# An MLP whose first group has three chunks in the program's order, four early pieces in a Fourier stage, and staged first transfers

## The chip, the cores and the metric

The kernel runs on one core of one Trainium2 chip. The metric is device time in microseconds (us) of one execution of the whole program. TensorE does the matmuls, VectorE and ScalarE the elementwise work (both can read PSUM), GpSimd (POOL) elementwise work in SBUF, and SyncE (SP) and ScalarE issue most DMA transfers. Each engine has one queue of instructions and works them off in order; engines wait for each other through semaphores.

## The reference

Three blocks are computed one after the other, for batch B = 4, S = 576 positions, 8 heads of 64, so a model width of 512. All inputs and the output are float32.

```python
# attention with a bias from relative positions
psi_rel = log1p(abs(pos[:, None] - pos[None, :]))
psi_i = log1p(maximum(pos[:, None], 1.0))
h = maximum((psi_rel / psi_i)[..., None] @ w1 + b1, 0.0)      # 32 hidden
scores = q @ k^T / 8 + (h @ w2).transpose(2, 0, 1)
x = softmax(scores) @ v                                        # [B, S, 512]
# Fourier mixing, normalisation, MLP
u = x + real(fft(fft(x, axis=1), axis=2))
mu = mean(u); var = mean((u - mu) ** 2)
un = (u - mu) / sqrt(var + 1e-06)
x = u + maximum(un @ w_ch1, 0.0) @ w_ch2                       # 512 -> 2048 -> 512
# gated block
h = maximum(x @ w_in, 0.0); a, v = halves of h
v_s = w_spatial @ normalised(v) + b_spatial
out = (a * v_s) @ w_out
```

## The kernel before, in words

One program does the three blocks in stages. Matmuls that need float32 accuracy are done on split operands: x = hi + lo in a fast 32-bit format, and hi*hi + hi*lo + lo*hi are accumulated, so that one product is three matmuls.

**Bias stage** (`bias_phase`, 0 to about 137 us). 48 blocks of three groups of four positions. For each group a 0/1 mask [128, 576] is made, on one of three ways (`ROUTE`): by TensorE and ScalarE from chunks of `c_xb` (X), by VectorE (D) or by POOL and VectorE (P) from `win` and `bn`. `make` makes a mask three blocks ahead, `collect` multiplies masks with `g` on TensorE, `evict` scales with `xt` and adds. `xscale` scales `xt` in place, 72 columns at every fourth block. The first transfers are issued at the top: `w`, a first `c_xb` chunk, `bn` and the two parts of `xt` on SP, `win` on ScalarE's queue. `win` is scaled by VectorE (L212) before the first D and P masks.

**Attention stage** (to about 433 us). At its end `first_folds` lets VectorE and ScalarE begin the folds for the Fourier stage: up to two steps for each round, up to step `F_MAX`. A batch has six steps, numbered on through the batches.

**Fourier stage** (`fft_phase`, about 422 to 518 us). For each batch b and parity e: `stage1` multiplies folded rows with cosine and sine tables (tile y, copied from PSUM by ScalarE, L826), `second` multiplies the copies (tile D, copied as d), `residual` transposes every second column of x on TensorE (tile xs, L843), and VectorE adds both into `ut` (L859, and `mirror`, L866). `step()` is called between these parts; it counts, takes one fold step, and, where `XPLAN` says so, one step of `extra`, the generator `early` of `tail`: preparing the first MLP weights and the mean of chunk 0. This stage and the one before stand under `manual_schedule`, which keeps the order of the program on each engine; elsewhere the scheduler of the language chooses an order.

**MLP stage** (`mlp_phase`, about 519 to 962 us). The 2304 positions are nine chunks of 256 (`MC`); the hidden width is 16 blocks (f) of 128. An item is one (f, chunk): 12 matmuls into `h` (L1227), `gh` = relu on ScalarE (L1231), `gl` = the rest on VectorE (L1232), and, two items later (`LAGF`), 12 matmuls into the chunk's `acc` (L1263). Chunks come in groups: (0, 1), then single ones, then (7, 8). A group's closing pieces multiply `acc` by the chunk's factor and add it to `ut` (L1273, L1274). `h` rotates over three PSUM tiles, and the statistics have a fourth tile, `st`.

A chunk must be normalised: `means` (three adds and a matmul with ones), `center`, `split` (uh, ul), `squares`, and `factor` (a matmul with ones, L1157, and the root). These are generators; an item takes some of their steps. In the first group the 32 weight tiles of 512 KB come in as well. `Weights.step` moves each weight in flight on by one: a transfer into one of three stage buffers, two steps later a ScalarE copy `wsq` (L958), then three VectorE integer passes (L962, L966, L969) that make a float32 from 64-bit input, then `wh` on ScalarE (L974) and `wl` on POOL (L975). Four weights (`N_EARLY` = 2 blocks) are made early. The stage buffers also hold a chunk's centred values `uc` while it is normalised.

**Gate stage** (to 1178 us). Its weights are prepared in the MLP's last group, through `later`.

Of the kernel before, what the change touches and what calls it, by code (L numbers as in the profile page):

```python
# [104 lines left out]
def bias_phase(tc, nc, io, vs, bias, biasl, early, es):  # L105
# [106 lines left out]
    nc.vector.tensor_scalar(out=win, in0=win, scalar1=w1p, scalar2=None, op0=ALU.mult)  # L212

# [456 lines left out]
F_MAX = 9  # L670
YB = 2
XPLAN = {10: 1, 14: 1, 30: 1, 31: 1, 32: 1}
# [125 lines left out]
def fft_phase(tc, nc, folds, tabs, ut, bank, extra, es):  # L798
# [35 lines left out]

    def residual(b, e, y):

        x = xs[b]
# [36 lines left out]
    def step():  # L874
# [3 lines left out]
        for _ in range(XPLAN.get(count, 0)):  # L878
            next(extra, None)
# [4 lines left out]
    for b in range(B):  # L884
        for e in range(2):
# [4 lines left out]
            for n, nm in enumerate(group):  # L890
# [3 lines left out]
                step()  # L894
                if n == 1:
# [91 lines left out]
LAGF = 2  # L987
MC = 256
# [97 lines left out]
class Norm:  # L1086
# [17 lines left out]
    def means(self, c, bank, stage, keep=None):  # L1104

        nc, u = self.nc, self.chunk(c)
        self.uc[c] = self.room(stage)
        s = self.uc[c][:, 0]
# [8 lines left out]
        if keep:  # L1117
            self.mean[c] = self.pool.tile([128, MC], F32, tag=keep, name="mu", bufs=1 + (keep == "rs"))
            nc.scalar.activation(out=self.mean[c], in_=m, func=AF.Copy)
            if keep == "rs":  # L1120
                self.scale[c] = self.mean[c]
        yield

    def center(self, c):

        uc, u = self.uc[c], self.chunk(c)
# [4 lines left out]
    def split(self, c, pool):  # L1131

        nc, uc = self.nc, self.uc[c]
        uh = pool.tile([128, 4, MC], F32R, tag="uh", name="uh", bufs=2)
        ul = pool.tile([128, 4, MC], F32R, tag="ul", name="ul", bufs=2)
# [17 lines left out]
    def factor(self, c, bank):  # L1153
# [4 lines left out]
        if c not in self.scale:  # L1158
            self.scale[c] = self.pool.tile([128, MC], F32, tag="rs", name="rs", bufs=2)
# [7 lines left out]
def mlp_phase(tc, nc, io, ut, norm, W, wts, later, es):  # L1167
# [11 lines left out]
    for _ in zip(norm.center(0), norm.split(0, lp)):  # L1179
        pass  # L1180

    for group in [(0, 1)] + [(c,) for c in range(2, NCH - 2)] + [(NCH - 2, NCH - 1)]:
        first, last = 0 in group, NCH - 1 in group
        pair = len(group) == 2
        c = group[-1] + 1

        def before():

            for x in group:
                if x != group[0]:  # L1190
                    yield from norm.means(x, bank, wts.stage)
                    yield from norm.center(x)
                    yield from norm.split(x, lp)
# [13 lines left out]
        if pair:  # L1207
            n = N_EARLY
            items = [(f, 0) for f in range(n)] + [(f, 1) for f in range(n)] + items[2 * n : -4]
            items += [(f, x) for x in range(2) for f in range(NF - 2, NF)]  # L1210
        acc = [ps_c.tile([128, len(group), MC], F32, tag=f"acc{d}", name="acc") for d in range(4)]
        gs = {}
        for i in range(len(items) + LAGF):
            if i < len(items):
# [7 lines left out]
                h = ps_h.tile([128, 512], F32, tag="h", name="h")  # L1222
                n = 0
                for k in range(4):
                    q = slice(128 * k, 128 * k + 128)
                    for st, mv in ((w1h, uh), (w1h, ul), (w1l, uh)):
                        nc.tensor.matmul(out=h[:, 0:MC], lhsT=st[:, q], rhs=mv[:, k], start=(n == 0), stop=(n == 11))  # L1227
# [3 lines left out]
                nc.scalar.activation(out=gh, in_=h[:, 0:MC], func=AF.Relu)  # L1231
                nc.vector.scalar_tensor_tensor(  # L1232
                    out=gl, in0=h[:, 0:MC], scalar=0.0, in1=gh.bitcast(F32), op0=ALU.max, op1=ALU.subtract
                )
# [450 lines left out]
```

## Time and profile before

| what | value |
|---|---|
| median of three runs | 1182.06 us (1177.35 to 1182.33) |
| the profiled execution's own time | 1180.53 us |
| its span, first to last instruction | 1178.6 us |
| TensorE matmuls busy | 1075.7 us, 91% of the span |
| VectorE busy | 716.2 us, 61% |
| ScalarE busy | 569.4 us, 48% |
| POOL busy | 379.0 us, 32% |
| mean granted TensorE clock | 0.974 |

The times of the trace are counted from the span's start. A busy share is that of the whole span and is made up of stages with different limits: the table by stretch below shows more. The granted clock is that which TensorE was allowed, as a share of 2.4 GHz; its other level is 1.2 GHz.

### The profile page before, as it was taken

Reading aid. Unit: us, or ns where it says so; the run is one execution under the profiler, and the core shown is the slowest. Engines: PE = TensorE matmul, PEld = TensorE weight load, DVE = VectorE, ACT = ScalarE, POOL = GpSimd, SP = SyncE. Lnnn points to the kernel's source line nnn. Section 1 sums busy time; section 2 is a strip of 40 time slices with the busy share of each in tenths; the row PEclk is TensorE's granted clock in tenths of the full one; section 3 lists DMA queues with packets and bytes.
Section 4 is the critical chain, followed back from the end, with each engine's and each line's share of the span. In section 5 each row is a group of like instructions: output and inputs, shape, how many; then the busy total and the mean of one; then the engine's idle time right before and its main releaser. Section 6 shows DMA issues by size and latency. Waiting matters only on the chain.

```text
span 1178.6 us, 25594 instructions
## 1 busy us (share of the span) xinstructions
PE 1075.7 (91%) x10519; PEld 989.0 (84%) x10519; DVE 716.2 (61%) x1887; ACT 569.4 (48%) x1056; POOL 379.0 (32%) x316
## 2 busy tenths in 40 slices
PE   4999898888988869989889999999999999999998
PEld 2778787777877757778779999999999999898997
DVE  4998877767877785579995242342567245443522
ACT  2888898798877623345542221221234224333332
POOL 2677687677777400014540000000014211101010
PEclk7999999989999969999999999999999999999999
DMA  6442088978998951015630000000214000101001
GB/s 153 162 131 96 12 168 180 165 166 171 184 169 159 201 168 37 1 37 171 187 108 1 1 1 1 1 1 1 73 37 147 11 1 1 37 1 45 1 36 45
DMA packets 142320, 96.34 MB, mean 82 GB/s; under 512 B 111416, under 2 KB 122812, under 8 KB 141948
## 3 DMA queue, kind: packets, MB, share of 16 engines
q1 hardware_dynamic: 139192, 85.85, 31.1%
q10 hardware_dynamic: 2724, 5.90, 1.7%
q0 software_dynamic: 288, 2.97, 0.7%
q8 instruction: 82, 1.34, 0.5%
q14 instruction: 34, 0.28, 0.1%
HBM read 58.42 MB, written 9.14 MB: 57 GB/s over the span
## 4 chain that ended last, share of the span: by engine, by line
PE 55%; DVE 18%; DMA 9%; ACT 5%; issue 5%; POOL 5%; SPq 1%; ACTq 0%; POOLq 0%; DVEq 0%
PE h L1227 14%; PE acc L1263 14%; PE psp L1398 5%; PE pu L1373 4%; PE po L1420 4%; DMA pt<-hl 3%; PE pv L1321 3%; PE sc L412 3%; POOL hl L464 2%; DMA raw<-in_k 2%; DVE wsq L966 2%; PE y L823 2%; DVE bt L308 2%; DMA win<-in_c_win 2%; DVE mask L232 2%
## 5 line engine op out<-in xcount | busy, mean ns | idle before, releaser
L975 POOL TENSOR_TENSOR wl<-wsq,wh 128x512 fp32r<-128x512 f32 x44 | 67.1, 1528 | 428.7 <-DVE w L1149 259.3
L1263 PE MATMUL acc<-gl,wh 128*128 128x256 f32 x576 | 162.8, 283 | 10.4 <-DVE gl L1232 10.0
L1263 PE MATMUL acc<-gh,wh 128*128 128x256 f32 x576 | 163.9, 286 | 2.7 <-ACT gh L1231 2.6
L1232 DVE SCALAR_TENSOR_TENSOR gl<-h,gh 128x256 fp32r<-128x256 f32 x144 | 60.2, 421 | 172.6 <-ACT gh L1231 172.5
L1227 PE MATMUL h<-uh,wh 128*128 128x256 f32 x576 | 162.9, 284 | 2.4 <-ACT uh L1137 2.4
L1227 PE MATMUL h<-uh,wl 128*128 128x256 f32 x576 | 162.9, 283 | 1.8 <-POOL wl L975 1.8
L1227 PE MATMUL h<-ul,wh 128*128 128x256 f32 x576 | 162.8, 283 | 0.6 <-DVE ul L1138 0.6
L1263 PE MATMUL acc<-gh,wl 128*128 128x256 f32 x576 | 161.8, 281 | 0.0
L1231 ACT ACTIVATE gh<-h 128x256 fp32r<-128x256 f32 x144 | 54.6, 380 | 213.9 <-PE h L1227 213.7
L518 PE MATMUL po<-vp,pt 128*128 128x65 f16 (+1 forms) x2240 | 95.6, 198 | 29.5 <-DMA pt<-hl 25.9
L1263 PEld LDWEIGHTS acc<-gl,wh 128*128 128x128 f32 x576 | 109.6, 190 | 13.3 <-DVE gl L1232 13.0
L464 POOL TENSOR_TENSOR hl<-P,hl 128x1024 f16<-128x1024 f32 x92 | 116.5, 1292 | 11.3 <-ACT hl L458 9.7
L518 PEld LDWEIGHTS <-pt 128*128 128x128 f16 (+1 forms) x2240 | 81.8, 103 | 44.3 <-DMA pt<-hl 31.4
L1227 PEld LDWEIGHTS h<-uh,wh 128*128 128x128 f32 x576 | 111.1, 193 | 3.4 <-ACT uh L1137 3.2
L1263 PEld LDWEIGHTS acc<-gh,wh 128*128 128x128 f32 x576 | 109.5, 191 | 4.7 <-ACT gh L1231 4.3
L1227 PEld LDWEIGHTS h<-uh,wl 128*128 128x128 f32 x576 | 110.7, 192 | 2.2 <-POOL wl L975 2.2
L1227 PEld LDWEIGHTS h<-ul,wh 128*128 128x128 f32 x576 | 110.7, 192 | 0.9 <-DVE ul L1138 0.8
L1263 PEld LDWEIGHTS acc<-gh,wl 128*128 128x128 f32 x576 | 109.6, 190 | 0.1
L447 ACT ACTIVATE P<-s,mm 128x576 f32<-128x576 f32 x144 | 103.3, 765 | 7.1 <-DVE mm L440 6.6
L425 DVE CUSTOM_DVE_ANT_0 s<-sc,lowb 128x576 f32<-128x576 f32 x80 | 60.6, 757 | 30.7 <-PE sc L412 26.6
L264 PE MATMUL bps<-g,mask 128*128 128x64 f16 x1152 | 61.6, 195 | 17.7 <-DVE mask L319 11.7
L247 ACT ACTIVATE mask<-pre 128x576 f16<-128x576 f32 x96 | 60.9, 651 | 31.2 <-PE pre L244 29.8
(247 smaller groups left out, 2778.8 us busy)
## 6 DMA issues: line engine op xcount, KB each, us to landing
w<-in_w_ch SPq DMA_DIRECT2D x32, 512.0 KB, 3.5
vld<-in_v ACTq DMA_DIRECT2D x16, 320.0 KB, 3.0
raw<-in_v SPq DMA_DIRECT2D x16, 320.0 KB, 3.4
raw<-in_q SPq DMA_DIRECT2D x16, 288.0 KB, 3.7
raw<-in_k SPq DMA_DIRECT2D x16, 288.0 KB, 6.0
w<-in_w_in SPq DMA_DIRECT2D x8, 512.0 KB, 3.5
out<-o SPq DMA_DIRECT2D x16, 256.0 KB, 2.0
xd<-x SPq DMA_DIRECT2D x15, 256.0 KB, 7.5
```

Of the source, the lines that this page charges most:

```text
L247: nc.scalar.activation(out=m.rearrange("p (x e) -> p x e", x=2), in_=p[:, :, 0:288], func=AF.Sigmoid, scale=1e30)
L264: nc.tensor.matmul(out=full(ps, it // 2)[:, it % 2, :, gi], lhsT=ms[gi][:, 128 * it : 128 * it + 128], rhs=g[:, k], start=(k == 0), stop=( ...
L425: nc.vector.tensor_tensor_reduce(out=s.rearrange("p (x e) -> p x e", x=2), in0=sc[:, :, 0:288], in1=bv.rearrange("p (x e) -> p x e", x=2), ...
L447: nc.scalar.activation(out=P[:, x], in_=s, func=AF.Exp, bias=mm[:, 1, x : x + 1], scale=1.0)
L464: nc.gpsimd.tensor_tensor(out=hl[:, :, o : o + c], in0=P[:, :, j : j + c], in1=hl[:, :, j : j + c], op=ALU.subtract)
L518: nc.tensor.matmul(out=po[c, t % 4, 0:w], lhsT=pt[:, x, c], rhs=vp[:, j, hh, f : f + w], start=(i == 0), stop=(i == len(seq) - 1),)
L975: nc.gpsimd.tensor_tensor(out=lo, in0=w[4], in1=hi.bitcast(F32), op=ALU.subtract)
L1227: nc.tensor.matmul(out=h[:, 0:MC], lhsT=st[:, q], rhs=mv[:, k], start=(n == 0), stop=(n == 11))
L1231: nc.scalar.activation(out=gh, in_=h[:, 0:MC], func=AF.Relu)
L1232: nc.vector.scalar_tensor_tensor(out=gl, in0=h[:, 0:MC], scalar=0.0, in1=gh.bitcast(F32), op0=ALU.max, op1=ALU.subtract)
L1263: nc.tensor.matmul(out=acc[d][:, x], lhsT=st[:, q], rhs=mv, start=(i == LAGF and n == 0), stop=(i == len(items) + LAGF - 1 and n == 2),)
L1398: nc.tensor.matmul(out=p[:, 0:CH], lhsT=st, rhs=mv, start=(n == 0), stop=(n == len(seq) - 1))
```

## The change

1. **First transfers.** At the top only the first 72 columns of `xt` are requested. The other 504 columns and the second `c_xb` chunk are issued further down, after the scaling of `win`: a memset of xt's last column, which stands behind that scaling on VectorE, makes the transfer wait.
2. **Fourier stage.** `F_MAX` is 5 instead of 9. `extra` is taken one step at every count from 8 on (`X_FIRST`), and `early` first makes the four weights and then the means of the first three chunks, each kept in its own tile. From the fourth (b, e) on, `gather` copies the columns that `residual` will transpose into contiguous room, on ScalarE.
3. **MLP.** The first group has three chunks (`TOGETHER`) and stands under `manual_schedule`. Norm steps are taken eight at an item for the first six items; a weight is started at item 0, then at two of three items up to 15, then at each. `h` has two PSUM tiles of two halves: blocks 0 and 1 of three in the one, block 2 and the statistics in the other. `acc` is two tiles for each chunk, over six tags in turn. The closing pieces go by chunk.

```diff
-    for k in (slice(0, 72), slice(72, S)):
-        nc.sync.dma_start(out=xt[:, :, k], in_=io["c_x"][:, :, k])
-    fill(1)
+    nc.sync.dma_start(out=xt[:, :, 0:72], in_=io["c_x"][:, :, 0:72])
...
     nc.vector.tensor_scalar(out=win, in0=win, scalar1=w1p, scalar2=None, op0=ALU.mult)
+
+    nc.vector.memset(xt[:, :, S - 1], 0.0)
+    nc.sync.dma_start(out=xt[:, :, 72:S], in_=io["c_x"][:, :, 72:S])
+    fill(1)
...
-F_MAX = 9
+F_MAX = 5
-XPLAN = {10: 1, 14: 1, 30: 1, 31: 1, 32: 1}
+X_FIRST = 8
...
+    room = xs[0].rearrange("p t f -> p (t f)")
+    parts = {}
+
+    def gather(b, e):
+
+        n = 2 * b + e
+        if 3 <= n < 2 * B:
+            o = 1280 * (n % 2)
+            t = parts[n] = room[:, o : o + 1280].rearrange("p (t s c) -> p t s c", t=5, s=2)
+            for s in range(2):
+                col = 257 + e if s else e
+                nc.scalar.activation(out=t[:, :, s], in_=xs[b][:, :, col : col + 255 : 2], func=AF.Copy)
...
-                nc.tensor.transpose(t[:, s, 128 * n : 128 * n + r], x[0:r, k, c], ident[0:r, 0:r])
+                i = x[0:r, k, c] if near is None else near[0:r, k, s]
+                nc.tensor.transpose(t[:, s, 128 * n : 128 * n + r], i, ident[0:r, 0:r])
...
-        for _ in range(XPLAN.get(count, 0)):
+        if count >= X_FIRST:
             next(extra, None)
...
                 step()
+                if n == 0:
+                    gather(b + e, 1 - e)
...
+TOGETHER = 3
...
-    def center(self, c):
+    def center(self, c, stage=None):
+        if c not in self.uc:
+            self.uc[c] = self.room(stage)
...
-    ps_h = es.enter_context(pool(tc, name="ps_h", bufs=3, space=PSUM))
+    ps_h = es.enter_context(pool(tc, name="ps_h", bufs=1, space=PSUM))
     ps_c = es.enter_context(pool(tc, name="ps_c", bufs=1, space=PSUM))
-    ps_l = es.enter_context(pool(tc, name="ps_l", bufs=1, space=PSUM))
+    halves = [ps_h.tile([128, 2, MC], F32, name=f"h{x}") for x in range(2)]
+    hs = [halves[0][:, 0], halves[0][:, 1], halves[1][:, 0]]
     def bank():
-        return ps_l.tile([128, 512], F32, tag="st", name="st")
+        return halves[1][:, 1]
...
-    for group in [(0, 1)] + [(c,) for c in range(2, NCH - 2)] + [(NCH - 2, NCH - 1)]:
+    for group in [tuple(range(TOGETHER))] + [(c,) for c in range(TOGETHER, NCH - 2)] + [(NCH - 2, NCH - 1)]:
+        es1 = ExitStack()
+        if 0 in group:
+            es1.enter_context(tc.manual_schedule())
...
-        acc = [ps_c.tile([128, len(group), MC], F32, tag=f"acc{d}", name="acc") for d in range(4)]
+        acc = {}
+        for x in range(several):
+            for z in range(2):
+                acc[x, z] = ps_c.tile([128, 2, MC], F32, tag=f"acc{turn % (2 * TOGETHER)}", name="acc")
+                turn += 1
...
-                h = ps_h.tile([128, 512], F32, tag="h", name="h")
+                h = hs[i % 3]
...
-                busy = pair and not (group[1] in norm.scale and group[1] not in norm.uc)
-                for _ in range(4 if busy else 1):
+                busy = several > 1 and not (group[-1] in norm.scale and group[-1] not in norm.uc)
+                for _ in range(8 if busy and i < 2 * several else 4 if busy else 1):
                     next(todo, None)
                 if first:
-                    wts.step(not busy or i < 2)
-                    while not busy and wts.busy() and (min(f + WLEAD, NF - 1), x) not in W:
-                        wts.step()
+                    wts.step(i == 0 or i > 2 and (i % 3 != 2 or i > 15))
...
     def early():
-        for _ in range(2):
-            wts.step()
-            yield
-        yield from norm.means(0, bank[0], wts.stage, "mu")
-        while len(W) + wts.wants() < 2 * N_EARLY:
+        while len(W) < 2 * N_EARLY:
             wts.step(len(W) + len(wts.flight) < 2 * N_EARLY)
             yield
+        for c in range(TOGETHER):
+            yield from norm.means(c, bank[0], wts.stage, f"mu{c}")
```

## Rows read from the trace of the kernel before

**Rows 1.** Busy time by stretch: PE, PEld, DVE, ACT, POOL, clock, DMA share, GB/s
```profile
24.50:31.10 6.60, 6.58 (x84) 5.08 (x84) 4.91 (x12) 2.92 (x5) 1.23 (x1) 0.52 0.04 14
440.40:492.00 51.60, 51.30 (x275) 40.53 (x276) 32.13 (x55) 16.95 (x34) 2.59 (x2) 0.97 0.07 21
519.00:636.40 117.40, 101.64 (x778) 96.35 (x779) 101.74 (x172) 53.98 (x112) 43.76 (x28) 0.97 0.38 117
636.40:865.40 229.00, 229.00 (x1943) 228.45 (x1942) 87.58 (x231) 47.44 (x128) 0.00 (x0) 1.00 0.03 10
865.40:962.00 96.60, 94.31 (x779) 93.44 (x778) 48.42 (x96) 36.69 (x82) 29.28 (x27) 0.98 0.20 60
...
519.00:540.00 21.00, 17.69 (x122) 16.51 (x123) 19.48 (x45) 12.47 (x29) 4.11 (x3) 0.92 0.26 76
```

**Rows 2.** Chain that ended last, first 40 us: start, length, what
```profile
1.69 18.37 DMA win<-in_c_win
...
20.08 0.83 DVE win L212
...
24.52 0.39 PE bps L264 x4
...
36.07 0.69 DVE xt L217
```

**Rows 3.** DMA view of the first 40 us: rate in 40 slices
```profile
GB/s 0 17 141 268 340 208 229 235 222 229 215 167 204 177 205 173 190 191 266 261 113 105 108 97 90 39 5 0 16 0 0 0 0 46 282 8 16 88 290 390
```

**Rows 4.** Timeline 428 to 441, VectorE, ScalarE, TensorE: start, length, what, idle before
```profile
428.45 1.48 DVE L746 TENSOR_TENSOR lowb<-lowb 128x1280 f32<-128x1280 f32 x1
429.96 0.82 DVE L753 TENSOR_TENSOR raw<-lowb 128x635 f32<-128x635 f32 x1
...
432.69 0.35 DVE L533 TENSOR_SCALAR ri<-po,vs 128x4 f32<-128x4 f32 x2
...
430.90 0.74 ACT L755 ACTIVATE fhi<-raw 128x640 fp32r<-128x640 f32 x1 [4.31 <-DVE raw L754]
...
440.36 0.85 PE L823 MATMUL y<-tt,fhi 128*128 128x290 f32 x2 [4.28 <-ACT y L826]
```

**Rows 5.** Timeline of the Fourier stage, VectorE and TensorE
```profile
456.76 0.76 DVE L859 TENSOR_TENSOR lowa<-xs,d 128x578 f32<-128x578 f32 x1 [3.70 <-ACT d L857]
...
470.49 0.76 DVE L859 TENSOR_TENSOR lowa<-xs,d 128x578 f32<-128x578 f32 x1
...
491.87 1.40 PE L843 MATMUL xs<-ident,lowb 128*128 128x128 f32 x6 [0.16 <-DVE lowa L859]
```

**Rows 6.** Timeline of TensorE: transposes of strided and of contiguous columns
```profile
457.76 1.34 PE L843 MATMUL xs<-ident,raw 128*128 128x128 f32 x6
...
403.14 0.74 PE L487 MATMUL turn<-ident,P 128*128 128x128 f32 x5
```

**Rows 7.** Groups by line, 519 to 636.4 us: busy, mean ns, idle before
```profile
L969 DVE SCALAR_TENSOR_TENSOR wsq<-w,wsq 128x512 int32<-128x512 int32 x28 | 38.4, 1370 | 0.5
L966 DVE SCALAR_TENSOR_TENSOR wsq<-w,wsq 128x512 int32<-128x512 int32 x28 | 20.3, 725 | 0.6
L962 DVE TENSOR_SCALAR wsq<-wsq 128x512 int32<-128x512 int32 x28 | 13.2, 472 | 1.0 <-ACT wsq L958 0.9
...
L975 POOL TENSOR_TENSOR wl<-wsq,wh 128x512 fp32r<-128x512 f32 x28 | 43.8, 1563 | 59.9 <-ACT wh L974 59.9
...
L974 ACT ACTIVATE wh<-wsq 128x512 fp32r<-128x512 f32 x28 | 17.7, 634 | 36.1 <-DVE wsq L969 36.0
```

**Rows 8.** Timeline of one item in a single-chunk group
```profile
700.97 0.28 PE L1227 MATMUL h<-uh,wl 128*128 128x256 f32 x1
...
701.70 0.42 DVE L1232 SCALAR_TENSOR_TENSOR gl<-h,gh 128x256 fp32r<-128x256 f32 x1 [2.29 <-ACT gh L1231]
```

**Rows 9.** Timeline: a matmul of statistics, and four norm pieces in a row
```profile
524.67 0.59 PE L1157 MATMUL st<-w,ones 128*128 128x256 f32 x2
...
693.89 1.40 DVE L1128 TENSOR_TENSOR w<-lowa,st 128x256 f32<-128x256 f32 x4
```

More of the change, by code (lines that the diff above doesn't have):

```diff
@@ L1106, in means @@
         nc, u = self.nc, self.chunk(c)
-        self.uc[c] = self.room(stage)
-        s = self.uc[c][:, 0]
+        t = self.room(stage)
+        s = t[:, 0]
+        if not keep:
+            self.uc[c] = t
         nc.vector.tensor_tensor(out=s, in0=u[:, 0], in1=u[:, 1], op=ALU.add)
@@ L1170, in mlp_phase @@
     gp = es.enter_context(pool(tc, name="mg", bufs=LAGF + 1))
-    ps_h = es.enter_context(pool(tc, name="ps_h", bufs=3, space=PSUM))
+    ps_h = es.enter_context(pool(tc, name="ps_h", bufs=1, space=PSUM))
     ps_c = es.enter_context(pool(tc, name="ps_c", bufs=1, space=PSUM))
-    ps_l = es.enter_context(pool(tc, name="ps_l", bufs=1, space=PSUM))
+    halves = [ps_h.tile([128, 2, MC], F32, name=f"h{x}") for x in range(2)]
+    hs = [halves[0][:, 0], halves[0][:, 1], halves[1][:, 0]]
     def bank():
-        return ps_l.tile([128, 512], F32, tag="st", name="st")
+        return halves[1][:, 1]
     NCH = B * S // MC
-    for _ in zip(norm.center(0), norm.split(0, lp)):
+    for _ in zip(norm.center(0, wts.stage), norm.split(0, lp)):
         pass
-    for group in [(0, 1)] + [(c,) for c in range(2, NCH - 2)] + [(NCH - 2, NCH - 1)]:
+    turn = 0
+    for group in [tuple(range(TOGETHER))] + [(c,) for c in range(TOGETHER, NCH - 2)] + [(NCH - 2, NCH - 1)]:
+        es1 = ExitStack()
+        if 0 in group:
+            es1.enter_context(tc.manual_schedule())
         first, last = 0 in group, NCH - 1 in group
-        pair = len(group) == 2
+        several = len(group)
         c = group[-1] + 1
         def before():
[L1189 to L1193, printed above, removed]
+            for x, y in zip(group, group[1:] + (None,)):
+                if y is not None:
+                    if y not in norm.mean:
+                        yield from norm.means(y, bank, wts.stage)
+                    yield from norm.center(y, wts.stage)
+                    yield from norm.split(y, lp)
                 yield from norm.squares(x)
@@ L1206, in mlp_phase @@
         items = [(f, x) for f in range(NF) for x in range(len(group))]
[L1207 removed]
+        if several > 1:
             n = N_EARLY
[L1209 to L1211 removed]
+            items = [(f, x) for x in range(several) for f in range(n)] + items[several * n : -2 * several]
+            items += [(f, x) for x in range(several) for f in range(NF - 2, NF)]
+        acc = {}
[3 more added lines that the diff above has]
+                turn += 1
         gs = {}
@@ L1226, in mlp_phase @@
                     for st, mv in ((w1h, uh), (w1h, ul), (w1l, uh)):
-                        nc.tensor.matmul(out=h[:, 0:MC], lhsT=st[:, q], rhs=mv[:, k], start=(n == 0), stop=(n == 11))
+                        nc.tensor.matmul(out=h, lhsT=st[:, q], rhs=mv[:, k], start=(n == 0), stop=(n == 11))
                         n += 1
@@ L1263, in mlp_phase @@
                         nc.tensor.matmul(
-                            out=acc[d][:, x], lhsT=st[:, q], rhs=mv,
-                            start=(i == LAGF and n == 0), stop=(i == len(items) + LAGF - 1 and n == 2),
+                            out=acc[x, d // 2][:, d % 2], lhsT=st[:, q], rhs=mv,
+                            start=(e == 0 and d % 2 == 0 and n == 0), stop=(e == NF - 1 and d % 2 == 1 and n == 2),
                         )
@@ L1268, in mlp_phase @@
                     later(e)
-        for d in range(4):
-            for x, cc in enumerate(group):
-                p = acc[d][:, x]
+        es1.close()
+        for x, cc in enumerate(group):
+            for d in range(4):
+                p = acc[x, d // 2][:, d % 2]
                 o = ut[:, d, MC * cc : MC * cc + MC]
```

21 lines of the change are left out of this document (10 added, 11 removed).

## The prediction

> **What bounds the kernel now.** I read the page first: TensorE is busy 91% of the span, so a gain has to come from stretches where it waits or runs at the lower clock. The table of busy time by stretch gives these [rows 1]. From 636.4 to 865.4 us TensorE never waits: 80 items (one hidden block of one chunk, 24 matmuls) in 229.0 us, 2.862 us an item, 1.43 us for its h half and 1.43 for its acc half. From 519.0 to 636.4 it does 32 items, which at that pace are 91.6 us, in 117.4, and VectorE is busy 101.7 of these: 25.8 us lost. The last pair, 865.4 to 962.0, loses 5. From 440.4 to 492.0 it is busy 51.3 of 51.6 us. Ahead of the MLP the chain of waits shows two more places: TensorE's first real work starts at 24.52 us, behind a transfer of win that takes 18.37 us [rows 2]; and at 440.36 us it has waited 4.28 us for ScalarE's copy of y [rows 4]. The change reaches all three.
>
> **Staged first transfers.** win shares the DMA engines with the rest of xt (1260 KB) and the second chunk of c_xb. After the change those wait for a VectorE memset that stands behind the scaling of win. What is left ahead of it (w, wx, bn, win, the first c_xb chunk, 72 columns of xt) is by their shapes about 1690 KB; adding up the DMA rate us by us, that much had moved by 9.3 us [rows 3]. So win lands near 9.8 and its scaling runs near 10.4, behind that of bn, instead of 20.08: 9.7 us. All that follows (POOL's z, the compare, TensorE's start 4.44 us after the scaling) moves with it. TensorE's pause then is 2 us instead of 11.6, and the stretch 24.5 to 31.1, where the granted clock was 0.52 (mostly its lower level of 1.2 GHz), should run higher; there VectorE's 4.9 busy us of 6.6 become the bound [rows 1]: 1.7 us more. Against it: the rest of xt now starts near 12 us, with two c_xb chunks behind it; 2412 KB at the 220 KB per us of these rows are 11 us, so it lands by 23. Block 4's scaling of xt asks for it: at 36.07 before, 11.5 us after TensorE's start [rows 2], so at 14.8 + 11.5 - 1.7 = 24.6. That is little cover, with v's loads beside it; I charge 0.6. Sum 9.7 + 1.7 - 0.6: **-11** (bounds -4, if VectorE stands 7 us waiting for xt, and -12).
>
> **Fourier stage.** F_MAX 5 takes four of batch 1's fold steps out of the attention tail: two sums of 1.48 us and two pieces of 2.73 (429.96 to 432.69), 8.4 us of VectorE [rows 4]. ScalarE waits 4.31 us for one of them, and the copies of y, for which TensorE waits, stand behind it in its queue. So TensorE should be 8.5 us earlier in batch 0. But the steps are not gone: they move behind, and the four early weights, of which two were prepared in gaps before this stage, now have their turn at counts 8 to 15, in batch 1. There VectorE has no room: from the output add at 456.76 to that at 470.49 it never waits for long, and the next transposes start right after such an add (at 491.87 even 0.16 us late) [rows 5]. Before the second add stand three weights now, each three integer passes of 0.47, 0.73 and 0.69 to 1.37 us [rows 7], with POOL's subtraction beside them 2.4 on average: 7.2 us. So of 8.5 about 1 is left at 471, and, with the means' adds (nine of 0.35 us) in the queue, nothing at 492. The last 27 us hold no folds, so there TensorE's own work counts: gather makes the transposed columns contiguous. Six strided transposes take 1.34 us, a pitch of 0.21; five of contiguous columns in the attention stage 0.74, a pitch of 0.117 [rows 6]: 0.57 us for a call of residual, five such calls that show after 492: 2.9. One more mean matmul costs 0.59 [rows 9]. The ten ScalarE gathers lie beside waits of ScalarE; uncovered they would cost 7. Sum **-2.5** (bounds -9, if weights and folds fit; +4, if neither the tail's gain nor the gathers show).
>
> **MLP, first group.** Three chunks make 48 items, 137.4 us, for the same 28 weights. VectorE's work: 28 weights of 2.45 (their three rows with the overlap of neighbours) are 69, 48 gl of 0.37 18, normalising chunks 1 to 3 some 51 pieces of 0.35, 18: 105 us, so VectorE is no longer the bound over the group. What is lost lies in the order.
>
> *Items 0 to 5.* In the program's order the factor matmul (st) stands in TensorE's queue between h and acc, and waits for that chunk's squares; eight norm steps follow each item. Count from the end of the first h, with VectorE pieces at 0.35 us [rows 9] and gh, gl ending 0.87 us after h [rows 8]. The first st waits for gh, then gl, 4 centers, 4 subtractions, gl, 3 adds (0.45 + 13 x 0.35): ready at 5.0 us, TensorE, with one h done, at 2.35: 2.7 lost. It ends at 5.6. The second waits for 18 more pieces (6.3) and ScalarE's root with handovers (2.3, an estimate): ready 14.2; TensorE, after the read of st, h, acc and h, at 10.4: 3.8. The third, from 14.8, for 10 pieces and one weight (3.5 + 1.7): ready 20.0, TensorE, after acc and h, 17.7: 2.3. With three st of 0.6 and 1.4 us for shared banks (below) 12 us are lost, where before the first 21 us held 122 matmuls, some 14 us of work [rows 1].
>
> *Weights at a fixed pace.* Up to f = 7 the step that ends a weight comes in the item just before its first use: ScalarE's wh (0.63) after gh, then POOL's wl (1.56) [rows 7] end 2.3 to 2.7 us after h, while the next h wants wl at 1.43 + 0.24 = 1.67: about 0.9 us, five times: 4.5. From item 16 one weight an item keeps VectorE at 2.45 + 0.37 = 2.82 of 2.862 us: 1.5 us for jitter.
>
> Its first h runs at the lower clock, as before (0.92 granted over the first 21 us, 1.7 us lost). So the group takes 137.4 + 1.7 + 12 + 4.5 + 1.5 = 157.1 us. The same three chunks took 117.4 + 45.8 = 163.2: -6.1.
>
> *h in shared banks.* h had three tiles; now blocks 0 and 1 of three lie in one tile and block 2 in another with the statistics. If accesses of two engines to one bank must take turns, every third h waits until gl of the one before has been read: 0.87 us after its end, with an acc half of 1.43 between: 0.56 us of room [rows 8]. Where VectorE is free it costs nothing; a group's start has no acc between, and there it costs up to 1.2 us. I take 1 us for the first group's end and 3 for the five later groups (none if tracked by bytes). MLP -6.1 + 4: **-2** (bounds -20, with the second case and no such waits, and +16, with the first).
>
> The Trainium skill, "PSUM — Partial Sum Buffer", section "PSUM bank collisions raise a hardware error", says that two engines must not be in one bank and quadrant at once, even at different columns, so such accesses have to be ordered by bank. No row of before shows h and gl in one bank; by that rule the waits are there, and without it the sum would be some 5 us lower.
>
> **Sum.** The profiled execution took 1180.53 us: 1180.5 - 11 - 2.5 - 2 = 1165. Its time is 1.5 us under the median of the three runs, so I say **1166**.
>
> **Rivals.**
> 1. *VectorE is late where banks are shared (not faster).* For: between 519 and 636 VectorE was 87% busy, and three pieces of a weight (2.5 us) can stand ahead of a gl. From the point where gl ends over 1.43 us after its h, every third h waits. Price: 1 us at each of 7 such items from 16 to 36 and 5 in the last group, 12; the first group's 24 closing pieces (8.3 us) ahead of the next gl, 5; four later starts of 1.2, 5; less the 4 charged: +18, 1184. Against: gl comes before the weight's pieces in each item, and the later groups are free to be ordered around it.
> 2. *TensorE isn't held at the start (faster still).* If adds and squares run ahead further than one piece per 0.35 us lets me count, the first six items lose 4 instead of 12, and wl is in time: -13, 1153. For: the pair lost only 7 there. Against: one queue, one order.
> 3. *xt comes too late (the staging doesn't do what it says).* The loads of v, 320 KB each, and the second and third c_xb chunk share the engines with it; if it lands at 30 us, 6 to 7 us of the 11 are gone: 1173. Against: the rate above.
>
> **Chances.** Forecast (1157 to 1177) 0.52; first rival (1176 to 1195) 0.16, second 0.20, third 0.12. Under 0.5%, some 6 us, a measurement here can't tell from no change. Faster by more than that (under 1176): 0.50 + 0.20 + 0.08 = 0.78; within it (to 1188): 0.02 + 0.09 + 0.04 = 0.15; slower 0.07, all from the first rival. The range leaves out about a tenth on either side: 1147, inside the second rival's case, to 1181, inside the first's.
>
> **What would show it.** Right: scaling of win near 10.4 and the first compare-fed matmuls near 15; xt's second scaling without a long wait; the copy of y no longer 4 us late; the output add of batch 1 behind three weights' passes; st in TensorE's queue with waits of 2 to 4 us, three times; the first acc of the fourth chunk some 156 to 160 us after the first h. Wrong: VectorE waiting for xt over 3 us in block 4; h waiting for gl in the single-chunk groups (229.0 us for five chunks becoming over 46.5 a chunk); or first items without waits for st.

## The result and the profile after

The changed kernel takes 1192.9 us (median of four runs, 1191.1 to 1194.7) where the kernel before, beside it, takes 1182.2: a ratio of 1.0096, 95% interval 1.0068 to 1.0125. It is slower by about 1%; 1166 was forecast. The profiled execution took 1191.71 us with a span of 1189.9.

The program has four seams that are easily found in any trace: TensorE's first mask product, its first product with the single column p1 (the Fourier stage begins), the first h of the MLP, and the first pv of the gate stage. The stretches between them, read from the timelines (from the first mask product to p1 the executions profiled here differ by up to 9 us, 397.7 to 406.7, where the code is the same, so that the stages are compared and not the ends):

| us | before | forecast | after |
|---|---|---|---|
| to the first mask product | 24.5 | 14.8 | 18.2 |
| from it to p1 | 398.0 | 397 | 397.7 |
| p1 to first h | 96.4 | 93.9 | 101.0 |
| first h to pv (MLP) | 442.1 | 440 | 456.1 |
| pv to the end | 217.6 | 217.6 | 217.0 |

The start's gain is smaller than forecast, the Fourier stage's is a loss, and 14 us are lost in the MLP. Rows of after, first by stretch (columns as in [rows 1]):

```profile
18.20:24.80 6.60, 6.60 (x98) 5.20 (x98) 5.41 (x14) 3.04 (x6) 1.69 (x2) 0.68 0.84 330
448.80:516.89 68.09, 55.05 (x288) 40.52 (x286) 38.00 (x63) 25.95 (x50) 6.47 (x4) 0.90 0.06 16
516.89:551.40 34.51, 24.02 (x128) 22.23 (x129) 20.53 (x54) 13.88 (x36) 1.28 (x1) 0.75 0.11 31
551.40:599.00 47.60, 43.32 (x361) 41.61 (x359) 28.49 (x48) 16.76 (x35) 11.78 (x9) 1.00 0.37 112
599.00:653.00 54.00, 48.91 (x410) 47.62 (x410) 51.45 (x69) 26.69 (x51) 30.11 (x17) 1.00 0.49 147
686.10:871.60 185.50, 184.79 (x1553) 184.08 (x1552) 69.00 (x180) 38.62 (x103) 0.00 (x0) 1.00 0.04 12
871.60:972.95 101.35, 94.49 (x777) 93.12 (x775) 50.23 (x100) 36.37 (x82) 26.90 (x27) 0.98 0.19 57
```

The first row answers to 24.50:31.10 before: granted clock 0.68 instead of 0.52. The second is the Fourier stage from D of (1, 0) (the product D of batch 1, parity 0) to the first h: TensorE idle for 13 of 68 us. The same stretch of before, with 1.7 us idle:

```profile
464.22:518.95 54.73, 53.05 (x284) 40.75 (x282) 31.38 (x51) 18.68 (x38) 2.99 (x2) 1.00 0.06 20
```

The third is the first six items of the MLP: 34.5 us, clock 0.75. In the fifth VectorE is busy 51.45 of 54 us, with 17 weights and 17 gl: 3.03 us for a weight and a gl. The last pair, 96.6 before [rows 1], takes 101.4.

**Start.** VectorE's timeline of after, and the DMA view of 7 to 13 us (the line DMA is the busy share of the 16 engines in tenths, in 40 slices):

```profile
13.76 0.82 DVE L210 TENSOR_SCALAR win<-win,w 128x1148 f32<-128x1148 f32 x1 [3.40 <-DMA win<-in_c_win]
...
28.89 0.77 DVE L219 TENSOR_SCALAR xt<-xt,gs 128x360 f32<-128x360 f32 x1
```
```profile
DMA  3303212403223312223213221332212321022100
...
DMA packets 254, 0.52 MB, mean 87 GB/s; under 512 B 149, under 2 KB 149, under 8 KB 254
...
q10 hardware_dynamic: 108, 0.48, 20.9%
```

The scaling of win comes at 13.76 instead of 20.08 [rows 2], not at 10.4. The second scaling of xt waits for nothing. From 7 to 13 us, just before win is there, it is nearly alone (q10: 0.48 of 0.52 MB) and moves at only 80 KB per us (87 with the rest), with 20.9% of 16 engines' time: as much as 3.3 engines.

**Fourier stage.** Timelines of after, three engines:

```profile
455.02 0.43 DVE L981 TENSOR_SCALAR wsq<-wsq 128x512 int32<-128x512 int32 x1
455.48 0.69 DVE L985 SCALAR_TENSOR_TENSOR wsq<-w,wsq 128x512 int32<-128x512 int32 x1
456.21 0.69 DVE L988 SCALAR_TENSOR_TENSOR wsq<-w,wsq 128x512 int32<-128x512 int32 x1
...
459.22 1.27 DVE L760 TENSOR_TENSOR fhi<-lowb,fhi 64x128 fp32r<-64x128 f32 x1
...
462.30 0.75 DVE L876 TENSOR_TENSOR lowa<-xs,d 128x578 f32<-128x578 f32 x1
```
```profile
463.09 0.64 ACT L879 ACTIVATE d<-D 1x580 f32<-1x580 f32 x1 [2.69 <-DVE lowa L876]
463.64 0.61 ACT L993 ACTIVATE wh<-wsq 128x512 fp32r<-128x512 f32 x1
464.16 1.46 ACT L849 ACTIVATE raw<-lowb 128x640 f32<-128x640 f32 x2
```
```profile
464.98 1.80 PE L860 MATMUL xs<-ident,raw 128*128 128x128 f32 x6 [9.24 <-ACT raw L849]
```

To here the transition had worked: D of (1, 0) began at 448.80 instead of 464.22, 6.6 us of it by the earlier start and 8.8 in this stage (32.9 us from p1 instead of 41.7). Then TensorE waits 9.24 us for a gather, which stands in ScalarE's queue behind the second copy of d, which waits for VectorE's output add, which stands behind the passes of three weights (one of them is shown) and two folds. Two smaller waits follow: 1.81 us at 476.62, for VectorE's adds, before the matmul of a mean, and 1.99 before the first h (1.38 before). D of (1, 0) to the first h takes 68.1 us, before 54.7 (518.95 - 464.22).

**MLP.** Waits of TensorE, 517 to 686 us and then 686.1 to 973:

```profile
PE h L1179 <- DVE w L1171: 8.8, 3, 3.1
PE h L1261 <- POOL wl L994: 4.7, 5, 1.3
PE h L1261 <- DVE gl L1266: 4.4, 6, 0.9
PE h L1261 <- ACT uh L1159: 2.0, 1, 2.0
...
PE h L1261 <- DVE gl L1266: 6.7, 3, 3.9
PE h L1179 <- DVE w L1183: 0.8, 1, 0.8
```

Each line gives the total, the number of waits and the longest. L1179 is the matmul of statistics in its shared tile: three waits of 2.6 to 3.1 us. After the first group, only h waiting for gl counts.

### The profile page after: what moved, and what is told of

It reads as the page before. It is cut to its first block, busy times and chain, and to the rows that moved or that the text cites. A ratio compares the mean times of both kernels' runs of the same rounds, so it can differ in the third digit from the quotient of the medians.

```text
span 1189.9 us, 25620 instructions
## 1 busy us (share of the span) xinstructions
PE 1079.8 (91%) x10519; PEld 990.1 (83%) x10519; DVE 718.4 (60%) x1888; ACT 576.6 (48%) x1068; POOL 379.0 (32%) x316
## 4 chain that ended last, share of the span: by engine, by line
PE 47%; DVE 12%; issue 3%; ACT 3%; POOL 1%; DMA 1%; DVEq 0%; ACTq 0%; POOLq 0%; SPq 0%
PE h L1261 14%; PE acc L1296 12%; PE psp L1432 5%; PE pu L1407 4%; PE po L1454 4%; PE pv L1355 3%; PE y L825 3%; DVE wsq L985 2%; DVE wsq L988 2%; PE D L872 2%; DVE wsq L981 1%; PE xs L860 1%; DVE gl L1266 1%; POOL wl L994 1%; DMA w<-in_w_in 1%
## 5 line engine op out<-in xcount | busy, mean ns | idle before, releaser
L1261 PE MATMUL h<-uh,wh 128*128 128x256 f32 x576 | 166.2, 289 | 15.0 <-DVE gl L1266 11.1
```

The source lines that it names most:

```text
L1261: nc.tensor.matmul(out=h, lhsT=st[:, q], rhs=mv[:, k], start=(n == 0), stop=(n == 11))
```

## The experiments

Ratios are to the kernel before, beside it on the same chip. Where a kernel has one profiled run, its stages are compared.

**1. The staged transfers alone.** The kernel before with the first two parts of the diff above (`xt` in two transfers, the second behind the memset).

> The kernel before with the staged first transfers alone. Theory A (what the profile of after shows at the start is a lasting gain, and everything else lost it): TensorE's first mask product starts at about 18.2 us instead of 24.5, each later stage is 6 to 7 us earlier, the end too: 1175 to 1176 us. Rival B (the rest of xt, landing later, or the lower clock takes some of it back by the end of the stage): under 3 us of gain, 1179 or more. The forecast's step said 11 us: 1171.

Measured: 1176.7 us, ratio 0.9925 (0.9897 to 0.9953); first mask product at 18.38, p1 to first h 97.4, MLP 443.5. The gain lasts: theory A. Its 9 us (0.0075 of 1182) have an interval of 5.6 to 12, so the trace's 6.1 are the better number.

**2. No gathers.**

```diff
-        if 3 <= n < 2 * B:
+        if False:
```

> The changed kernel with the strided columns transposed directly in all calls (no gather copies on ScalarE). Theory Q (ScalarE's queue holds the gather, so the gather itself makes the 9.2 us pause of TensorE at 456 to 465): the pause falls to 1 or 2 us, and the first h of the MLP comes 6 to 8 us sooner, near 509. Theory V (VectorE, with twelve passes of four weights in its queue, is late, and the gather only stands behind it): the transposes still wait for the output add that frees the tile xs at 463.1, a pause of 7 to 7.5 us; with 0.2 to 0.5 us more for each strided call the first h stays within 1.5 us of 517.

Measured: D of (1, 0) to first h 68.5 us, against 68.1 with gathers; in place of the wait for the gather stands

```profile
470.11 1.84 PE L860 MATMUL xs<-ident,lowb 128*128 128x128 f32 x6 [7.38 <-DVE lowa L876]
```

the wait for VectorE that theory V gave in advance (7 to 7.5). The first h itself came at 524.3, outside what either theory said, because the attention stage of this execution was 6.6 us longer.

**3. The early weights later.**

```diff
-X_FIRST = 8
+X_FIRST = 20
```

> The changed kernel with X_FIRST 20 instead of 8: the four early weights' VectorE passes come at counts 23 to 26, when no folds are left, and the means after them. Theory V (VectorE is overfull where weights and folds fall together): the pause of 9.2 us before 465 shrinks below 2, the stretch to the last D is shorter by 6 to 9; the means that are not reached cost up to 2 at the MLP's start: first h near 510 to 512. Theory Q (the gather on ScalarE's queue): the pause stays above 6 us.

Measured: D of (1, 0) to first h 60.7 us; 7.4 less, as theory V said. But two waits for a gather are left, 1.50 us at 461.82 and 3.03 at 486.18, so theory Q has a smaller part. All three means were still made in the stage, their matmuls from 482.6 to 507.5, and the MLP took 456.3, the same.

**4. Weights last and no gathers.**

```diff
-X_FIRST = 8
+X_FIRST = 23
...
-        if 3 <= n < 2 * B:
+        if False:
```

> The changed kernel without gathers and with X_FIRST 23: the passes of the four weights come in batch 2, after its folds, and most means after the stage. From D of (1, 0) to the first h the kernel before took 54.7 us, the changed one 68.1, that without gathers 68.5, that with X_FIRST 20 60.7. Theory V (VectorE's overlap of folds and weights, and nothing else, makes the loss): 54.5 to 57 us. Rival (the two more means and the weights cost TensorE and ScalarE wherever they are put, and contiguous columns do help): 59 or more.

Measured: 55.0 us, as theory V said, with two waits of TensorE of 0.3 us in all, and 0.8 before the first h. The three means were made in the stage here too (matmuls from 503.9 to 508.4), so that they are not the loss. The whole loss of 13.4 us is weights among the folds and gathers, and they cover each other: weights without gathers cost 13.5 (68.5 - 55.0), gathers with late weights 5.7 (60.7 - 55.0, with X_FIRST 20 against 23; 6.5 at 23 in both, experiments 11 and 12).

**5. F_MAX alone**, on top of the staged transfers, everything else as before.

```diff
-F_MAX = 9
+F_MAX = 5
```

> The kernel before with the staged first transfers and F_MAX 5, weights, means and MLP as before. In the changed kernel and its variants the time from the first product with p1 to D of (1, 0) fell from 41.7 to 32.6 to 32.9 us. Theory F (this comes from F_MAX alone and is lasting where no weights stand in VectorE's queue): the time from D of (1, 0) to the first h stays within 2 us of 54.7, so the end is 7 to 9 us ahead of the version with the staged transfers alone: a ratio to the kernel before near 0.985 instead of 0.9925. Rival G (the folds that are left out of the tail are missing later, with weights or without): the second time grows by 5 or more, and the ratio stays above 0.990.

Measured: 1172.9 us, ratio 0.9886 (0.9863 to 0.9909): between what the two theories said, 0.985 and above 0.990. p1 to D of (1, 0) is 32.9 us (41.7 before), and D to the first h 58.1, 3.4 more than before: TensorE waits 1.96 us at 460.90 for an output add that stands behind two folds, and runs at the lower clock after it (0.68 granted from 460.9 to 465.4). So of 8.8 us 5.4 last here, and 8.5 in experiment 4, where the same folds made nothing late. The traces show what differs: the kernel before, and this one, make two weights in batch 0, and experiment 4 makes none there. VectorE's timeline of this run:

```profile
433.10 0.76 DVE L964 TENSOR_SCALAR wsq<-wsq 128x512 int32<-128x512 int32 x2
433.77 1.29 DVE L968 SCALAR_TENSOR_TENSOR wsq<-w,wsq 128x512 int32<-128x512 int32 x2
434.98 1.29 DVE L971 SCALAR_TENSOR_TENSOR wsq<-w,wsq 128x512 int32<-128x512 int32 x2
...
436.97 1.62 DVE L755 TENSOR_TENSOR raw<-lowb 128x635 f32<-128x635 f32 x1
438.51 1.24 DVE L756 COPY raw<-lowb 128x5 f32<-128x5 f32 x1
```

Counted from p1 the output add comes at 41.0 us here and at 38.9 in experiment 4: 2.1 us later, which is the wait. Theory F's condition, no weights in VectorE's queue, did not hold in this run; where it holds, in experiment 4, the gain lasts. That the folds are missing later even without weights, theory G, is not what experiment 4 shows.

**6. Tiles of their own for h after the first group.** Two tags of the first group's acc become h and statistics.

```diff
...
+        if first:
+            own = [ps_c.tile([128, 2, MC], F32, tag=f"acc{z}", name="own") for z in range(2)]
+            hs[1], stat[0] = own[0][:, 0], own[1][:, 0]
+            at = lambda n: 2 + (n - 6) % 4
```

> The changed kernel, but after the first group h rotates over three tiles of their own and the statistics have a fourth (two of the tags that the first group's acc used); the first group is as it was. From the first h of the MLP to the gate stage the changed kernel took 456 us. Theory S (h of two items in one tile makes TensorE wait for VectorE's gl, 6.7 us after the first group in three waits): the waits for gl there vanish, the five later groups take 5 to 7 us less. Rival R (the last pair loses through VectorE's and ScalarE's load of gate weights and norm steps, whatever tile h is in): less than 2 us, the waits turn into others.

Measured: MLP 447.5 us, 8.5 less: 9.3 less in the later groups, 0.8 more in the first. The four single chunks take 45.79 us each (46.28, 46.29, 45.89 and 47.20 in the changed kernel, 45.79 before), and the stretch of the last pair

```profile
869.02:963.63 94.61, 92.70 (x776) 91.53 (x776) 51.06 (x100) 35.74 (x82) 28.90 (x27) 1.00 0.20 61
```

VectorE has as much to do as in the changed kernel (51.06 and 50.23 us), and no h waits for gl. Theory S, and for more than the 5 to 7 us that it said.

**7. h alternating between the two tiles.**

```diff
-    hs = [halves[0][:, 0], halves[0][:, 1], halves[1][:, 0]]
+    hs = [halves[0][:, 0], halves[1][:, 0]]
-                h = hs[i % 3]
+                h = hs[i % 2]
```

> The changed kernel with h alternating between the two PSUM tiles (one half of each, statistics in the other half of the second) instead of three places in two tiles: h of an item then never shares a tile with the item just before it. Theory S (shared tiles): the waits of h for gl, 4.4 us in the first group and 6.7 behind it, vanish: MLP 445 to 449 us instead of 456. Rival P (VectorE alone sets the pace where one weight is made for each item: 51.5 us busy of 54 between 599 and 653): items 16 to 37 stay above 3.10 us each, and the first group gains less than 2.

Measured: MLP 452.7 us, 3.4 less. Items 16 to 37 took 64.9 us instead of 66.5, 3.09 us an item. From item 25 on each took these 3.09, where the changed kernel had 2.7, 2.7 and 3.8 in turn, and VectorE was as busy as there:

```profile
599.00:653.00 54.00, 52.44 (x434) 50.76 (x435) 51.49 (x69) 25.12 (x51) 30.15 (x17) 1.00 0.47 147
```

Rival P for this stretch (its bound was 3.10, and the first group gained 1.4 us): the wait in a shared tile was only where VectorE's pace showed. Of the five later groups, chunks took 46.5 us: the third tile is worth something too.

**8. Weights one item sooner.**

```diff
-                    wts.step(i == 0 or i > 2 and (i % 3 != 2 or i > 15))
+                    wts.step(i in (0, 3, 4) or i > 4 and (i % 3 != 1 or i > 15))
```

> The changed kernel with the weights of the first group started one item sooner from the fourth on (items 0, 3, 4, 5, 6, 8, 9, 11, ... instead of 0, 3, 4, 6, 7, 9, 10, ...). Theory J (wl and wh come just in time: each third item between 6 and 18 takes 4.4 us instead of 2.7 to 2.8): those thirds fall to below 3.2 and the first group is 4 to 6 us shorter. Rival: the loss only moves, because VectorE's passes of two weights now meet the norm steps of the first items or gl: gain under 1.5 us.

Measured: the thirds of 4.4 us became 2.7; items 6 to 16 took 29.5 us instead of 32.4, and 16 to 37 63.8 instead of 66.5: theory J. MLP 448.1; of the 8 us 5 are in the first group and 3 in the later ones, which the edit doesn't touch; why isn't settled.

**9. The scheduler's order in the first group.**

```diff
-        if 0 in group:
-            es1.enter_context(tc.manual_schedule())
```

> The changed kernel without the fixed program order in the MLP's first group: the scheduler of the language chooses it, as in the kernel before. Theory O (the program's order costs: the matmuls of statistics wait 8.8 us in TensorE's queue, VectorE's gl behind weights): the first group takes 160 us or less instead of 169. Rival: the scheduler puts weights ahead as in the kernel before, where the first sixteen items took 69 us against 65 now: the group takes 169 us or more.

Measured, with items by the starts of gh: items 0 to 6 19.1 us (32.7 in the program's order), 6 to 16 40.4 (32.4), 16 to 37 69.7 (66.5); MLP 452.3, the first group 165.9: between the 160 of theory O and the 169 of the rival. Each has a part, one after the other: the statistics no longer hold TensorE, then h waits 15.5 us for gl, which stands among the passes of weights in VectorE's queue, and of 13.6 us 3.8 stay.

**10. The MLP altered in three ways:** as in 6; weights as in 8 with `i > 27` for `i > 15`; in the first group the norm steps behind the acc half, and in `factor`

```diff
...
+        for _ in range(5 if c < TOGETHER else 0):
+            yield
         t = bank()[:, 0:MC]
```

> The changed kernel with its MLP altered in three ways: h and statistics with tiles of their own after the first group (as measured before, 8.5 us less); weights one item sooner (measured 4 us less in the first group) and two in three items up to item 27 instead of 15; in the first group the norm steps of an item behind its acc half and each statistics matmul five steps later, so that TensorE has an item more of work ahead of it. Theory O (the statistics matmul stands too early in TensorE's queue: 8.7 us in three waits; VectorE is the pace from item 16 on only because it makes a weight an item): those waits fall below 4 us in all, items 16 to 37 to 2.95 us or less, MLP from 456 to 433 to 437 us. Rival L (in the first six items VectorE's norm pieces are the bound, so that TensorE waits for something else instead): the first six items still take 30 us or more, the MLP 440 to 444.

Measured: MLP 434.4 us. Waits of TensorE from 524 to 682 us:

```profile
PE h L1266 <- DVE w L1185: 3.4, 2, 2.9
PE h L1266 <- ACT uh L1159: 3.2, 3, 2.0
PE h L1266 <- DVE ul L1160: 2.5, 2, 2.3
PE h L1266 <- DVE gl L1271: 2.3, 4, 0.9
...
```

No wait of the statistics' matmul is left; items 16 to 37 take 59.3 us, 2.82 each. The first six took 24.8 us instead of 32.7: theory O, though other waits (the read of st, uh, ul) keep them from the 16.1 us of work that they hold (ten halves of 1.43 and three st of 0.6), which is rival L's part.

**11 and 12. All repairs (4 and 10) in one kernel, without and with the gathers.**

> All repairs in one kernel: the changed kernel with X_FIRST 23, no gathers, and the altered MLP (own tiles behind the first group, weights sooner and two in three items to item 27, norm steps behind the acc half, statistics matmuls five steps later). If the terms add up as the stages were measured alone, against the kernel before: start 6.2 us less, transition to the Fourier stage 9, Fourier stage 0.3 more, MLP 7 less, together 22 us: ratio 0.981 (0.978 to 0.985). Rival: the Fourier stage's gain is given back at the MLP's start, because ten more steps of the means are left over for it: the MLP takes over 440 us instead of 435, ratio 0.986 or more.

> The same with the gathers. Theory C (with VectorE no longer late the contiguous columns give TensorE what the forecast said, about 0.3 us for each of the calls by the transposes of the changed kernel, 1.10 to 1.15 instead of 1.40 us): 1 to 2.5 us less than without. Rival Q (ScalarE's queue holds the gathers behind the weights' copies, as the waits of 1.5 and 3.0 us with X_FIRST 20 suggest): 1 to 4 us more than without.

Measured: 1160.2 us, ratio 0.9813 (0.9785 to 0.9841), without; 1166.0, ratio 0.9852 (0.9826 to 0.9878), with. p1 to first h 87.6 and 94.1, MLP 432.8 and 432.7. The terms add up, and the gathers cost 6 us at the end, 6.5 between p1 and the first h: rival Q, and for more than its 1 to 4. Two of the three waits for a gather come with no weight ahead of them. From ScalarE's and TensorE's timelines with gathers:

```profile
460.23 0.64 ACT L879 ACTIVATE d<-D 1x580 f32<-1x580 f32 x1 [1.00 <-DVE lowa L876]
460.78 1.45 ACT L849 ACTIVATE raw<-lowb 128x640 f32<-128x640 f32 x2
```
```profile
461.60 1.30 PE L860 MATMUL xs<-ident,raw 128*128 128x128 f32 x6 [1.50 <-ACT raw L849]
465.92 2.44 PE L872 MATMUL D<-y,fs 128*128 128x290 f32 x8
...
484.97 1.30 PE L860 MATMUL xs<-ident,raw 128*128 128x128 f32 x6 [2.05 <-ACT raw L849]
488.85 2.92 PE L872 MATMUL D<-y,fs 128*128 128x290 f32 x8
```

The gather stands behind a copy that waits for VectorE. These two waits are also paid twice: eight matmuls of D behind them take 2.44 and 2.92 us instead of 2.12, at the lower clock. The third wait, 1.42 us at 507.75 and not shown, is not: D behind it takes 2.12.

**13 and 14. win in four transfers,** in the repaired kernel and, alone, in the kernel before.

```diff
-    nc.scalar.dma_start(
-        out=win, in_=io["c_win"].rearrange("j (a i) -> j a i", a=1).to_broadcast([4, HID, WLEN])
-    )
+    for j in range(4):
+        nc.scalar.dma_start(
+            out=win[HID * j : HID * j + HID], in_=io["c_win"][j : j + 1].to_broadcast([HID, WLEN])
+        )
```

> The repaired kernel with the transfer of win issued as four, one for each of its four rows, each spread to 32 partitions. In the changed kernel, from 7 to 13 us, win was nearly alone (108 of 254 packets, 0.48 of 0.52 MB) and moved at 87 GB/s with a fifth of the 16 engines' time: 3.3 engines. Theory E (one transfer whose outermost dimension is 4 is confined to four engines, which is why win landed at 13.6 and not at 9.8 us): in four parts it uses all, lands at 9.5 to 10.5, TensorE's mask products start 3 to 4 us sooner, near 14.8, and the ratio to the kernel before falls from 0.981 to 0.978. Rival B (its packets or its source are slow whichever engines take them): it lands within 1 us of 13.6, the ratio stays.

> The kernel before with nothing changed but win issued as four transfers. Theory E (win's 18.4 us are those of four engines shared with xt and c_xb): with sixteen engines it takes its share sooner, its scaling comes at 14 to 17 us instead of 20.1, TensorE's first mask product 3 to 6 us sooner: 1177 to 1179 us where the kernel before takes 1182. Rival D (the queue behind: xt and c_xb hold the engines, so that only leaving them for later helps): scaling at 19 us or later, no change.

Measured: in the repaired kernel win is scaled at once behind bn,

```profile
10.46 0.82 DVE L211 TENSOR_SCALAR win<-win,w 128x1148 f32<-128x1148 f32 x1
```

the first mask product starts at 14.91, and the time is 1155.7 us, ratio 0.9776 (0.9752 to 0.9800). In the kernel before, alone, the scaling comes at 11.83 instead of 20.08, the first mask product at 16.27, and the time is 1178.1 us, ratio 0.9958 (0.9938 to 0.9978). Theory E in both; in the second, win came 2 us sooner than it said. There TensorE's first mask product comes 8.3 us sooner, and the end by the ratio 5.0 (2.6 to 7.3): a part of the gain is not kept, and no run shows where it goes.

## Why the prediction failed, step by step

**Start: mechanism right, -11 was -6.** The bytes ahead of win were as counted; the step that failed is the landing, "that much had moved by 9.3 us". It added up the rates of before, some 220 KB per us, which are those of a mix of transfers. With xt out of the way win is soon nearly alone, and then it moves at 80, with a fifth of the engines' time. Experiment 13 takes this away, and the scaling comes at 10.46, where the forecast had it. The Trainium skill, "DMA: Bandwidth & Descriptors", section "Rules for kernel authors", says that a transfer whose outermost dimension is smaller than 16 uses at most that many engines, and win's is 4; the 3.3 busy engines agree. The 1.7 us for the clock didn't show (0.68 granted and not 1), and the 0.6 for xt weren't needed: from the first mask product to the second scaling of xt 10.7 us, before 11.5 [rows 2].

**Fourier stage: -2.5 was +4.6.** The tail's 8.5 us were there, 8.8 by experiments 4 and 5. "So of 8.5 about 1 is left at 471" held for the output add itself: counted from p1 it came 1.6 us sooner than before (462.30 - 415.92 against 470.49 - 422.52 [rows 5]). What failed is the path behind it, where next to nothing was charged.
- The add ends at 463.05, but the transposes of the gathered columns start at 464.98, behind the copy of d and the gather in ScalarE's queue, and TensorE, after 9.24 us of waiting, runs at the lower clock (0.53 granted from 464.98 to 469.83). D of (1, 1) begins 53.9 us after p1, before 52.0.
- The second mean was charged 0.59 us for its matmul alone; the 1.81 us of waiting for VectorE's adds were not. D of (2, 0) begins 67.5 us after p1, before 62.2.
- "The ten ScalarE gathers lie beside waits of ScalarE" was the next mistake: what counts is what stands ahead of them in the queue. And the 0.57 us a call were taken from transposes of another stage; here a call takes 1.10 to 1.16 us where it took 1.29 to 1.40, some 0.2 less. From D of (2, 0) to the first h the stage gained 0.8, not 2.9. Where the weights stand late, the gathers cost 5.7 to 6.5 in all (experiments 3, 4, 12).

One reading was wrong too: the two weights "prepared in gaps before this stage" have their passes at 439.15 to 445.38 in the kernel before, in batch 0 of this stage. Experiment 5 shows what they cost there once the folds are moved. And the terms as written, -2.9 and 0.59, add up to -2.3 and not -2.5.

**MLP: -2 was +14.** By part (the 157.1 us forecast for the first group were 169.1, to the first h of the fourth chunk at 686.0):
- The three waits for statistics, forecast 2.7, 3.8 and 2.3, were 2.60, 3.12 and 3.05. The places are right; that the sum of 8.8 is exact is luck, one term being 0.7 under and another 0.7 over. wl just in time, forecast 4.5, was 4.7.
- Clock: this is one mis-sized term of the first group. The first six items took 34.4 us, to the seventh h at 551.25: 14.3 of work (six halves for h, four for acc), 1.8 for st, 10.5 of waits and 7.8 of lower clock, where 1.7 was charged, for the first h alone. Waits brought the lower clock back: 0.97 granted before the second wait for statistics, 0.61 behind it.

```profile
530.80:533.60 2.80, 2.80 (x25) 2.80 (x23) 2.28 (x7) 1.44 (x5) 0.00 (x0) 0.97 0.00 0
536.90:541.20 4.30, 4.25 (x21) 4.20 (x22) 2.93 (x6) 0.42 (x1) 0.00 (x0) 0.61 0.00 0
```

- "From item 16 one weight an item keeps VectorE at 2.45 + 0.37 = 2.82 of 2.862 us: 1.5 us for jitter" is the other. From item 18 to the fourth chunk the group took 96.4 us for 88.7 of work: 7.7 over, of which 2.2 are two of the waits for wl. From 599 to 653 a weight's three passes and a gl kept VectorE busy for 3.03 us, so that one weight an item does not fit into 2.862. At two weights in three items the loss vanishes (2.82 us an item, experiment 10), in other tiles it doesn't (experiment 7).
- h in shared tiles: 3 us charged for the five later groups; 9.3 measured (experiment 6), of which 6.8 in the last pair. This is the first rival, at the last of its places and near its price there (5, and 5 for later starts). Its 7 us for items 16 to 36 came too, some 6 (66.3 us for 60.1), but by VectorE's pace more than by the shared tile. The rule of the Trainium skill that the prediction cites, "PSUM — Partial Sum Buffer", section "PSUM bank collisions raise a hardware error", agrees: with h of neighbouring items in different tiles the waits are gone. No run tells an order kept by tile from one kept by bank.

The first rival, with 0.16, was the nearest, 1184, and the measured time lies in its range. That is in part luck: it had no price for the Fourier stage, for the start or for the clock, which together make more than half of the 27 us between 1166 and 1193. The second and third rivals are out: the first items were held, xt came in time. What the failed steps have in common: two costs were let lie beside each other (weights beside folds, gl beside weights) on an engine that the forecast had itself found to be full.

What stays open: the 3 us that the later groups gained in experiment 8, and the last eleven items of the first group with the two acc halves behind them, 36.9 us where 34.3 would do, also with all repairs.

## What to carry to other kernels

An engine that is busy 85 to 95% of a stage, as VectorE was here, is to be taken for a bound: work moved there is to be priced by what waits behind it in each queue that it passes, not by the gaps that an average shows. A copy that makes another engine's work shorter is worth it only if what stands ahead of it in its own queue is never late. And of a slow transfer, look at the share of the DMA engines when it is alone: if that is a fifth, as here, the form of the transfer may be the bound, and splitting it is to be tried beside clearing the way for it. Alone the split gave 5 us and the clearing 9, with intervals that overlap; on top of the clearing the split gave 4 more.

## What the runs showed of the hardware

- One transfer of 574 KB from four rows to 128 partitions moved, nearly alone, at 80 KB per us with 20.9% of 16 engines' time, as much as 3.3 of them; as four transfers it was there by 10.4 us at the latest instead of 13.7.
- VectorE's subtraction L760 of 64x128 takes 0.28 us alone and 1.27 to 1.29 while POOL makes wl (453.58 to 454.85 and 459.08 to 460.35):

```profile
453.58 1.27 POOL L994 TENSOR_TENSOR wl<-wsq,wh 128x512 fp32r<-128x512 f32 x1 [51.77 <-ACT wh L993]
459.08 1.27 POOL L994 TENSOR_TENSOR wl<-wsq,wh 128x512 fp32r<-128x512 f32 x1 [4.22 <-ACT wh L993]
```
```profile
447.13 0.28 DVE L760 TENSOR_TENSOR fhi<-lowb,fhi 64x128 fp32r<-64x128 f32 x1
453.71 1.29 DVE L760 TENSOR_TENSOR fhi<-raw,fhi 64x128 fp32r<-64x128 f32 x1
```

  It ends just behind POOL's instruction, as the Trainium skill, "SBUF — State Buffer", section "Who interferes with whom", has it: the ports that the two share are an exclusive lock, here for POOL's whole instruction.
- Short waits of TensorE can cost twice. In the repaired kernel with gathers the granted clock was 1.00 before a wait of 1.50 us (446 to 460) and 0.72 behind it (462 to 468); behind one of 2.05 us the eight matmuls of D took 2.92 us instead of 2.12, behind one of 1.42 us they took 2.12:

```profile
446.00:460.00 14.00, 14.00 (x79) 11.18 (x77) 10.61 (x20) 4.40 (x8) 0.00 (x0) 1.00 0.00 0
462.00:468.00 6.00, 5.93 (x28) 3.77 (x27) 1.06 (x1) 1.03 (x4) 0.00 (x0) 0.72 0.00 1
```
